# Forty projections of the first attention block on 64-row tiles that swap banks, with one pool of seven PSUM banks and a new order

## The chip, the cores and the metric

The kernel runs on one core of one Trainium2 chip. The metric is the device time of one execution in microseconds, taken as the median of several runs. A profile of one more execution (its "profiled execution") shows what each engine did: TensorE (PE, with its weight loads as PEld), VectorE (DVE), ScalarE (ACT), GpSimd (POOL) and the DMA queue that SyncE issues (SP).

## What is computed

Two independent attention blocks over 2048 tokens of 512 features with 32 heads of 16. Block A sees only the current token and the 255 before it; block B sees all tokens. The outputs stand side by side.

```python
def _A_ref(x, wqkv, wo):          # B, S, D = 1, 2048, 512; H = 32, Dh = 16, W = 256
    qkv = ...((x @ wqkv).reshape(B, S, 3, H, Dh))
    q, k, v = qkv[0], qkv[1], qkv[2]
    scores = jnp.einsum("bhqd,bhkd->bhqk", q, k) * (Dh ** -0.5)
    mask = (idx[:, None] - idx[None, :] >= 0) & (idx[:, None] - idx[None, :] < W)
    scores = jnp.where(mask[None, None], scores, -1e9)
    p = _softmax(scores, axis=-1)
    o = jnp.einsum("bhqk,bhkd->bhqd", p, v)
    return o.transpose(0, 2, 1, 3).reshape(B, S, D) @ wo
# _B_ref: the same without the mask
return jnp.concatenate([a, b], axis=-1)
```

## The kernel before

**Splitting.** Every float32 operand of a projection is held as a rounded part and a remainder (`split`, L136 to L138, or L263 and L264), and a product of two operands is three matmuls: rounded by rounded, rounded by remainder, remainder by rounded. A projection (`project_qk`, `project_v`) contracts 512 features in four pieces of 128 rows, so it is 12 matmuls of 128 x 512, all accumulating in one PSUM bank (`products`, L188). `ps_all` is the whole PSUM as eight banks of 512 columns.

**Layouts on TensorE.** Three layouts of the array occur. Projections use all 128 rows. Scores (L537) and row maxima (L426 for block A, L378 for block B) contract 48 or 51 rows, so two heads stand at partitions 0 and 64 (`ROW = 0, 64`) and run as pairs on two 64-row tiles, each into a bank of its own. Weighing with the values (L583 for A, L568 for B) has 17 output columns, and four heads stand on four 32-column tiles. The transpose of the row maxima (L504, 48 columns) is a fourth. These layouts are called modes below, and a stretch of instructions in one mode a stay.

**Block A's stage.** A loop reads `ORDER_A`, one letter a step: `p` a whole projection, `m` a maximum (two heads of one query tile), `s` scores of two heads, `w` a weighing, `t` the transpose of the finished maxima, `e` a maximum of block B done early. `ORDER_P` names the projections in order (`Aq01`: block A, queries of head group pair 0, token chunk 1; `Av13`: values of token tile 7). All 96 projections of queries, keys and values of both blocks are done in this stage. What else happens (loads, stores, splits) is put in by a planner, `Model`, that keeps a time for each engine and a release time for each bank; the order on each engine is then fixed in the program, and engines wait for one another by semaphores. The planner charges a `turn` when TensorE changes its mode.

**Banks.** Scores take single banks of a pool `e` of three; maxima take double banks of a pool `p` of two; the accumulator of weighings has one bank, `o`. Projections and transposes take `e`, or one half of a `p` before the scores begin. A bank comes free when ACT or DVE has read it: scores by the exponentials (L544), maxima by DVE (L435 then L436, or L382), projections by an ACT copy (L249, L253, L330).

**After a projection.** Queries and keys: ACT copies the bank to `raw` (L253), POOL splits it (L263, L264), SP stores it (L271), and later loads bring it to `oq` and `opk` in the layout of the scores. Values: ACT copies to `vst` (L330), SP stores (L338). Probabilities of block A are masked by POOL (L554) before they are weighed; scores run at most `AHEAD` = 3 steps ahead of weighings.

**Block B's stage** follows, with the fixed pattern `ORDER` of scores, maxima and weighings; `max_rows` (L504) occurs there too.

Of the kernel before, what the change touches and what calls it, by code (L numbers as in the profile page):

```python
# [20 lines left out]
HG = 4  # L21
# [7 lines left out]

NAMES = str.maketrans({"(": "", ")": "", ",": "", " ": "_", "'": ""})  # L30
# [15 lines left out]

ORDER_P = (
# [4 lines left out]
    "Bk12 Bk33 Bk31 Bk30 Bk11 Bq30 Bq13 Bq31 Bq20 Bk32 Bq32 Bq33 ").split()  # L52
# [6 lines left out]
    "ppppppppppmmpmmpmmpmmpmmpmmtppmmpmmspsmmptpmsmswsmmpmsmwsmptmmspmswmsmpsmwsmmpmswsmmpmsmwtsmmswsmpmm"  # L59
    "spmtmswmswsmmpsmwsmmswtmsmpsmwsmmpmswstmmspmswmsmswmsmpmsmwtswsmmswspsmmpmsmwmspsmmwsmtwsmmswmsmpsmw"  # L60
    "mstmpsmmswsmmswsmpsmmwtmspsmwsmmwmswmsmsmpmmswspmtpmsmwswmspmmspsmmstmwsmsmwmsmpmswmmpmsmtsmwmmspsmm"
    "wmstwmssmwmsmsmpmsmwtsmwsmmsmswmsmpmsmwsmsmmwtsmmswmspsmmwsmsmwsmmsptmwmsmpsmwsmmswtmspsmwmsptmmpsmm"
    "wswsmpsmwsmmpmsmwtsmmswmsmpsmmswmsmpmsmwtmswsmwmsmpsmmswsmmswtmsmswmsmpmmswsmpmswtmsmpmsmwsmpsmmwsmp"
    "msmwtsmmswsmpmmswsmpmswtmmspmswmmspmswsmmtpsmmwswesmpmsmwsmpsempesmwtmswmsmpmswmmspemspemtpsewsmmpsm"
    "mwsmpsemwspemspmsmwtsewmsmpsmmwtsesmpesmwsmpmswmsmpsmmwsmpmsmwwmmtpemspesmpesmpemswsmwmswsmmpsempmsm"
    "pmsmptmmwwwmm")
# [7 lines left out]
class Model:  # L74
# [14 lines left out]
    def pe(self, mode, ns, *after):  # L89

        turn = self.turn * (mode != self.mode)
        self.mode = mode
        return self.run("PE", turn + ns, *after)
# [25 lines left out]
def attention_kernel(ctx: ExitStack, tc: tile.TileContext, xT, wqk, wv, wo, out):  # L119
# [62 lines left out]
    def products(ps, pairs, start=True, stop=True):  # L182
# [3 lines left out]
        for l, r in pairs:  # L186
            for u, v in ((0, 0), (0, 1), (1, 0)):
                nc.tensor.matmul(ps, l(u), r(v), start=start and k == 0, stop=stop and k == n - 1)  # L188
                M.pe("f", 232)
# [9 lines left out]
    def view(bank):  # L199
        pool, n = bank  # L200
        first, width = {"e": (0, 1), "o": (3, 1), "p": (4, 2), "s": (6, 1)}[pool]
        n = first + width * n + (pool == "e" and n > 2)
        return ps_all[:, n] if width == 1 else ps_all[:, n:n + 2]

# [13 lines left out]
    def constants():  # L218
# [11 lines left out]
        for v in vt:  # L230
            nc.gpsimd.memset(v[:, :, VP:], 1.0)
# [7 lines left out]

    def project_qk(b, p, s, c):  # L240

        n = f"{b}_{p}_{s}_{c}"
        bank, ps = room()
        yield from products(ps, [(lambda u, i=i: ws[b, p, s][:, u, 128 * i:128 * i + 128], lambda v, i=i: xs[b, c, i][:, v])
                      for i in range(4)])
        at_most(project_qk, 1)
        two = sb.tile([128, 2, QC], F32R, name=f"st_{n}", tag="st")
        if (b, p) == (0, 0):
            nc.scalar.activation(two[:, 0], ps, AF.Copy)  # L249
            t1 = M.run("ACT", 480, M.t["PE"] + WAKE)  # L250
        else:
            raw = row(f"raw_{n}")
            nc.scalar.activation(raw, ps, AF.Copy)  # L253
            t1 = M.run("ACT", 480, M.t["PE"] + WAKE)
# [20 lines left out]
        after(t1, sub, (project_qk, b, p, s, c))  # L275

# [44 lines left out]

    def project_v(b, c, a):

        kt = 4 * c + a
        bank, ps = room()
        yield from products(ps, [(lambda u, i=i: xs[b, c, i][:, u, 128 * a:128 * a + 128], lambda v, i=i: ws[b, "v", i][:, v])
                      for i in range(4)])
        v = vst[0]
        vst.reverse()
        nc.scalar.activation(v[:, :, 0:DH], ps.rearrange("p (h d) -> p h d", d=DH), AF.Copy)  # L330
        t = M.run("ACT", 480, M.t["PE"] + WAKE)
# [35 lines left out]
    def max2(g, c, qt, kc, heads, ps):  # L367
# [14 lines left out]
        nc.vector.tensor_reduce(out=m[:, a:a + len(heads), r, qt, kc], in_=ps, axis=AX.X, op=ALU.max)  # L382
        return M.run("DVE", 65 + 533 * len(heads), t)
# [23 lines left out]
    def max_item(b, g, c, qt, j, kc):  # L407
        n = f"{b}_{g}_{c}_{qt}_{j}_{kc}"
        if b:
            pr = M.take("p")  # L410
            M.release(pr, max2(g, c, qt, kc, (j, j + 1), view(pr)))
            return
# [9 lines left out]
        bank = M.take("p")  # L422
        two = view(bank)
# [5 lines left out]
        if i < 2:  # L429
            for a in range(2):  # L430
                nc.vector.tensor_tensor_reduce(junk[:, :w], two[:, a, 0:w], wmask[:, 256 - w:], 1.0, -3.0e38,
                                               ALU.add, ALU.max, accum_out=m[:, a, r, qt, 0:1])
                t = M.run("DVE", w / 0.96 + 310, t)
        else:
            nc.vector.copy_predicated(two[:, :, 256:384], later, two[:, :, 0:128])  # L435
            nc.vector.tensor_reduce(out=m[:, :, r, qt, 0], in_=two[:, :, 128:384], axis=AX.X, op=ALU.max)  # L436
            M.run("DVE", 455, t)
            t = M.run("DVE", 610)
        M.release(bank, t)
# [25 lines left out]
    def max_finish(b, g, c):  # L465
# [13 lines left out]
        nm = sb.tile([128, 2, 3, HG // 2, 4], BF16, name=f"nm_{n}", tag="nm")  # L479
        parts["nm"] = nm  # L480
        nm = [nm[:, :, i].rearrange("p a r q -> p a (r q)") for i in range(3)]
# [259 lines left out]
    def bank():  # L741
        return M.bank(pool())
# [402 lines left out]
```

## Time and profile before

| | |
|---|---|
| runs | 1834.06 us median of 3 (1833.39 to 1835.33) |
| profiled execution | 1839.76 us, its span on the core 1838.0 us, mean granted TensorE clock 0.994 |
| TensorE busy in the span | 99% |
| block A's stage | from 0 to about 550 us |
| L188 projections of the whole run (`ps_all<-x,w` and `ps_all<-w_v,x`) | 768 and 384 matmuls, mean 408 and 399 ns |

A matmul's length in the profile covers its whole way through the array, and those that follow overlap it; the distance from start to start says what one costs in a row. So the timeline is read by its first column. The groups of instructions by line have, behind the bar, the idle time of the engine before them and what ended it.

### The profile page before, as it was taken

The page shows a single profiled execution, that of the slowest core. Times are in us where ns is not written, and L with a number is a line of the kernel's source. Part 1 is how long each engine was busy: PE and PEld are TensorE (multiplying, and loading weights), DVE is VectorE, ACT ScalarE, POOL GpSimd, SP SyncE. Part 2 cuts the span into 40 slices and gives each one's busy share as a digit, 9 for nine tenths or more (in the row PEclk, how much of TensorE's full clock was granted, in tenths as well). Part 3 has the DMA queues.
Part 4 walks back from the last instruction along what each step waited for, and adds up shares of the span by engine and source line. Part 5 has one row for each costly group of instructions (what it writes and reads, how often), then busy time and mean ns, then how long its engine had stood idle before and what let it go on. Part 6 is the DMA issues. An engine that isn't in the chain of part 4 may idle for free. (4 is left out here: it accounts for less than half of the span.)

```text
span 1838.0 us, 37676 instructions
## 1 busy us (share of the span) xinstructions
PE 1815.5 (99%) x14376; PEld 901.5 (49%) x14376; DVE 1530.6 (83%) x2275; ACT 1404.2 (76%) x2750; POOL 648.8 (35%) x1333
## 2 busy tenths in 40 slices
PE   8999999999999999999999999999999999999999
PEld 6666656666663544444444443444444434444436
DVE  4677677766778777799999999999999999999901
ACT  4366566665547777799999999999999999999983
POOL 0367878564662433032221022430013232122330
PEclk9999999999998999999999999999999999999999
DMA  8755656545554222411310032121031121010012
GB/s 261 206 178 184 208 183 197 165 151 158 167 174 108 85 84 84 98 29 34 63 37 17 23 74 49 28 63 30 17 75 29 34 63 36 17 49 12 32 36 92
DMA packets 129157, 166.72 MB, mean 91 GB/s; under 512 B 23012, under 2 KB 58852, under 8 KB 128964
## 3 DMA queue, kind: packets, MB, share of 16 engines
q1 hardware_dynamic: 128976, 164.31, 30.7%
q8 instruction: 113, 1.85, 0.4%
q14 instruction: 68, 0.56, 0.1%
HBM read 94.49 MB, written 68.19 MB: 89 GB/s over the span
## 5 line engine op out<-in xcount | busy, mean ns | idle before, releaser
L544 ACT ACTIVATE p<-ps_all 128x512 f32<-128x512 f32 x2432 | 1260.7, 597 | 161.1 <-PE ps_all L537 104.8
L382 DVE TENSOR_REDUCE mt<-ps_all 128x2 f32<-128x1024 f32 x1516 | 1195.1, 868 | 77.4 <-PE ps_all L378 73.4
L537 PE MATMUL ps_all<-oq,opk 51*128 51x512 f32 (+2 forms) x2752 | 783.6, 409 | 6.3 <-ACT p L544 5.4
L378 PE MATMUL ps_all<-opk,oq 48*128 48x512 f32 x2016 | 677.5, 440 | 2.1 <-DVE mt L382 1.9
L568 PE MATMUL ps_all<-p,vt 128*17 128x256 f32 (+1 forms) x6056 | 590.6, 462 | 0.5 <-ACT ou L594 0.5
L537 PEld LDWEIGHTS ps_all<-oq,opk 51*128 51x128 f32 x2752 | 400.2, 185 | 193.9 <-ACT p L544 170.8
L378 PEld LDWEIGHTS ps_all<-opk,oq 48*128 48x128 f32 x2016 | 310.3, 186 | 317.8 <-DVE mt L382 177.7
L554 POOL TENSOR_SCALAR_AFFINE_SELECT p<-p 128x256 f32<-128x256 f32 x480 | 179.8, 406 | 148.4 <-ACT p L544 141.8
L568 PEld LDWEIGHTS ps_all<-p,vt 128*17 128x17 f32 x6056 | 101.0, 95 | 225.0 <-issue 214.4
L188 PE MATMUL ps_all<-x,w 128*128 128x512 f32 x768 | 198.3, 408 | 7.1 <-ACT x L137 6.6
L453 POOL TENSOR_TENSOR mu<-mt 128x16 f32<-128x16 f32 x31 | 6.8, 220 | 509.6 <-DVE mt L382 509.6
L435 DVE COPY_PREDICATED ps_all<-mone,ps_all 128x256 f32<-128x256 uint16 x224 | 94.9, 424 | 90.7 <-PE ps_all L426 89.6
L188 PEld LDWEIGHTS ps_all<-x,w 128*128 128x128 f32 x768 | 143.5, 193 | 47.2 <-ACT x L137 6.8
L436 DVE TENSOR_REDUCE mt<-ps_all 128x2 f32<-128x512 f32 x224 | 155.3, 693 | 7.7
L622 POOL TENSOR_TENSOR rd<-ld,minus 128x32 f32<-128x32 f32 x15 | 81.9, 5457 | 220.6 <-DMA ld<-od 220.6
L253 ACT ACTIVATE raw<-ps_all 128x512 f32<-128x512 f32 x56 | 33.5, 598 | 106.5 <-PE ps_all L188 106.5
L583 PE MATMUL ps_all<-p,vt 128*17 128x384 f32 (+2 forms) x1408 | 95.8, 387 | 0.0
L188 PE MATMUL ps_all<-w_v,x 128*128 128x512 f32 x384 | 95.6, 399 | 0.0
L426 PE MATMUL ps_all<-opk,oq 48*128 48x384 f32 (+2 forms) x512 | 91.0, 376 | 2.4 <-DVE mt L436 2.2
L188 PE MATMUL ps_all<-w_o,x_o 128*128 128x512 f32 x384 | 92.8, 396 | 0.1
L188 PEld LDWEIGHTS ps_all<-w_o,x_o 128*128 128x128 f32 x384 | 70.6, 188 | 30.0 <-issue 13.6
L188 PEld LDWEIGHTS ps_all<-w_v,x 128*128 128x128 f32 x384 | 70.0, 188 | 18.7 <-issue 2.7
(72 smaller groups left out, 738.9 us busy)
## 6 DMA issues: line engine op xcount, KB each, us to landing
parts<-st SPq DMA_DIRECT2D x64, 512.0 KB
oq<-parts SPq DMA_DIRECT2D x128, 128.0 KB
opk<-parts SPq DMA_DIRECT2D x128, 128.0 KB
od<-ou SPq DMA_DIRECT2D x64, 256.0 KB
vd<-vst SPq DMA_DIRECT2D x32, 272.0 KB
oq<-parts SPq DMA_DIRECT2D x128, 64.0 KB
opk<-parts SPq DMA_DIRECT2D x128, 64.0 KB
t<-od SPq DMA_DIRECT2D x32, 256.0 KB
```

The costliest lines, as they stand in the source:

```text
L188: nc.tensor.matmul(ps, l(u), r(v), start=start and k == 0, stop=stop and k == n - 1)
L378: nc.tensor.matmul(ps[:, n], q[rows, 128 * qt:128 * qt + 128], k[rows, kc * QC:kc * QC + QC], start=True, stop=True)
L382: nc.vector.tensor_reduce(out=m[:, a:a + len(heads), r, qt, kc], in_=ps, axis=AX.X, op=ALU.max)
L426: nc.tensor.matmul(two[:, a, 0:w], opq[b, g, c][rows, r, 128 * qt:128 * qt + 128], opk2(g)[rows, r, t0:t1], start=True, stop=True)
L435: nc.vector.copy_predicated(two[:, :, 256:384], later, two[:, :, 0:128])
L436: nc.vector.tensor_reduce(out=m[:, :, r, qt, 0], in_=two[:, :, 128:384], axis=AX.X, op=ALU.max)
L537: nc.tensor.matmul(ps[x][:, col:col + n1], opk2(g)[rows, pr, 128 * k:128 * k + 128], opq[b, g, c][rows, pr, q0:q0 + n1], start=True, stop= ...
L544: nc.scalar.activation(p[:, a0 + x, :w], ps[x][:, :w], AF.Exp, scale=SCALE)
L554: nc.gpsimd.affine_select(out=v, in_=v, pattern=[[0, 2], [sign, 128]], compare_op=ALU.is_ge, fill=zero_fill, base=base, channel_multiplier ...
L568: nc.tensor.matmul(o[32 * j:32 * j + VW, q0:q1], vt[(g // 2) % 2][:, kt, vc:vc + VW], pts[1, g, c, kt, j // 2][:, j % 2, q0:q1], start=kt ...
L583: nc.tensor.matmul(o[32 * j:32 * j + VW, q0:q0 + w], vt[(g // 2) % 2][:, kt, vc:vc + VW], pts[b, g, c, m, j // 2][:, j % 2, col:col + w], ...
L622: nc.gpsimd.tensor_tensor(rd, ld, minus, op=ALU.pow)
```

## The change

**Pairs on 64-row tiles.** 40 of the 96 projections are no longer done one by one. Two are taken together (`g` in `ORDER_A`, 80 letters: four chunks for each of 20 pairs). A pair's products are cut in half along the contraction: in the first two chunks, rows 0 to 63 of the first projection run on the upper tile into the first bank, and rows 64 to 127 of the second on the lower tile into the second bank. In the last two chunks the halves are exchanged, so that each tile writes the other bank. One chunk is 6 steps of two matmuls, so a pair is 48 matmuls of 64 rows instead of 24 of 128. Other letters stand between the chunks.

**The wait at the swap.** The first matmul after the exchange is made to depend on the earliest eviction, by the planner's time, of anything that TensorE was given after the first half (`since`, `mark`).

**One pool.** `e` and `p` become one pool `u` of seven single banks; maxima and scores take any two (`take2`, read with a stride), projections and transposes one, a pair two from its first chunk to its evictions. In block B's stage the banks are as before.

**Transposes.** The maxima are kept 32 columns apart with zeros in the unused 8 (`nmt`), and two transposes of 32 columns replace one of 48, in both blocks; the copy behind them has 64 rows for 48.

**Small changes.** One of two constant margins (`vt[0]`) is dropped, the planner's `turn` has one value for each mode, and `ORDER_P` and `ORDER_A` are new throughout.

```diff
+CHUNK = 6
 ORDER_P = (
-    "Aq00 Aq01 Ak00 Av13 Av00 Av03 Aq02 Av20 Ak01 Av10 Av21 Ak02 Av02 Av33 Aq03 Av01 Ak03 Av12 Av11 Aq13 Aq10 "
+    "Aq00 Ak00 Av11 Av01 Aq01 Av03 Ak01 Ak02 Av13 Av12 Aq02 Av00 Aq03 Av02 Av10 Ak03 Av23 Ak11 Av32 Ak10 Av20 "
...
 ORDER_A = (
-    "ppppppppppmmpmmpmmpmmpmmpmmtppmmpmmspsmmptpmsmswsmmpmsmwsmptmmspmswmsmpsmwsmmpmswsmmpmsmwtsmmswsmpmm"
+    "pppppppppmmpmmppmmgmgmpmmgtmgmmpmmgsgmspsmgsmgmswtmmmppmsgsmgmmpsmgmmgmwtwmmspmsgmsgmswsgmsgmtwssmws"
...
-        self.mode, self.turn = "f", 170
-        self.banks = {"e": [0] * 3, "p": [0] * 2, "o": [0]}
+        self.mode, self.turn = "f", dict(f=210, h=200, c=139)
+        self.banks = {"u": [0] * 7, "o": [0]}
...
+    def take2():
+        banks = sorted(M.take("u") for _ in range(2))
+        i, j = (n + n // 3 - n // 6 for _, n in banks)
+        return banks, ps_all[:, i:j + 1:j - i]
...
+    nmt = [cst.tile([128, 2, 32], BF16, name=f"nm{i}") for i in range(2)]
-    vt = [cst.tile([128, NT, VP + 16], F32, name=f"vt{i}") for i in range(2)]
+    vt = [cst.tile([128, NT, VP + 16 * i], F32, name=f"vt{i}") for i in range(2)]
...
+    def mark(op, t):
+
+        since.append((t, len(since), op))
+        return t
+
+    def half_rows(stage, pairs, banks):
+
+        turn, q0 = divmod(CHUNK * stage, 12)
+        for q in range(q0, q0 + CHUNK):
+            k, i = divmod(q, 3)
+            u, v = ((0, 0), (0, 1), (1, 0))[i]
+            for a in range(2):
+                l, r = pairs[a ^ turn][k]
+                rows = slice(64 * a, 64 * a + 64)
+                op = nc.tensor.matmul(view(banks[a ^ turn]), l(u)[rows], r(v)[rows], start=turn == q == 0,
+                                      stop=turn == 1 and q == 11)
+                if turn and q == a == 0:
+                    tc.add_manual_dep(op.ins, min(since)[2].ins.name, LANDED, reason="the row tiles change banks")
+        M.pe("h", CHUNK * 233)
...
-        bank = M.take("p")
-        two = view(bank)
+        banks, two = take2()
...
-        nc.tensor.transpose(ps[:48, :128], nm.rearrange("p a s j q -> p (a s j q)"), ident)
-        nt = sb.tile([48, 128], F32, name=f"ntr_{n}", tag="ntr")
-        nc.scalar.activation(nt, ps[:48, :128], AF.Copy)
+        for a in range(2):
+            nc.tensor.transpose(ps[32 * a:32 * a + 32, :128], nm[:, a], ident)
+        nt = sb.tile([64, 128], F32, name=f"ntr_{n}", tag="ntr")
+        op = nc.scalar.activation(nt, ps[:64, :128], AF.Copy)
...
+        elif x == "g":
+            if stage == 0:
+                two = its_a[nb:nb + 2]
+                nb += 2
+                banks = [M.take("u") for _ in range(2)]
+            half_rows(stage, [(pairs_qk if f == project_qk else pairs_v)(*a) for f, *a in two], banks)
+            stage += 1
+            if CHUNK * stage == 12:
+                since.clear()
+            elif CHUNK * stage == 24:
+                stage = 0
+                for (f, *a), bank_ in zip(two, banks):
+                    (end_qk if f == project_qk else end_v)(*a, bank_, view(bank_))
+                    made.add((f, *a))
```

The order on TensorE shows the change best. The rows are line, operation, output and inputs, columns, and the repeat count. First the program before, early in block A's stage: whole projections (L188) of 12 matmuls between maxima (L426) and a transpose (L504).

```order
L426 MATMUL ps_all<-opk_73,oq_0_1_254 128x384 x4
L188 MATMUL ps_all<-x_3_0_308,w_0_0_113 128x512 x3
L188 MATMUL ps_all<-x_3_1_311,w_0_0_113 128x512 x3
L188 MATMUL ps_all<-x_3_2_325,w_0_0_113 128x512 x3
L188 MATMUL ps_all<-x_3_3_328,w_0_0_113 128x512 x3
L426 MATMUL ps_all<-opk_73,oq_0_1_254 128x384 x4
L504 LDWEIGHTS nm_0_0_451
L504 MATMUL ps_all<-ident,nm_0_0_451 48x128
L188 MATMUL ps_all<-w_v_160,x_0_0_116 128x512 x3
```

After the change, about the same place: the end of a pair's first chunk, one maximum (now L474), and the second chunk (L314); both projections' operands alternate.

```order
L314 MATMUL ps_all<-x_3_1_297,w_0_0_116 128x512
L314 MATMUL ps_all<-w_v_181,x_0_1_122 128x512
L474 MATMUL ps_all<-opk_75,oq_0_0_231 128x384
L474 MATMUL ps_all<-opk_75,oq_0_0_231 128x384 [waits Activation_49]
L314 MATMUL ps_all<-x_3_2_312,w_0_0_116 128x512 [waits DVE_49]
L314 MATMUL ps_all<-w_v_190,x_0_2_127 128x512
```

The same projection of chunk 3 with `w_0_0`, one stay in the full array before, now shares its tiles' mode with the maxima beside it, in pieces.

Later in block A's stage, after the change: the swap of a pair, with the two narrow transposes (L553), scores (L586) and an early maximum of block B (L427) between the halves. The bracket names the engine whose result the first matmul of the second half waits for.

```order
L314 MATMUL ps_all<-w_v_3820,x_2_3_3196 128x512
L553 LDWEIGHTS nm_74
L553 MATMUL ps_all<-ident,nm_74 32x128
L586 MATMUL ps_all<-oq_6_2_4905,opk_75 128x256 [waits Activation_49] x2
L586 MATMUL ps_all<-oq_6_2_4905,opk_75 128x256 x2
L427 MATMUL ps_all<-vt_77,qe 128x512 x2
L314 MATMUL ps_all<-w_v_3579,x_2_0_3055 128x512 [waits Activation_49]
L314 MATMUL ps_all<-x_3_0_3320,w_2_0_4304 128x512
```

Before, no instruction waited for an eviction of another bank in this way, and a transpose never stood between the parts of a projection.

The end of the stage, before: two maxima of block B (L378, two pairs of matmuls), the first scores of block B (L537), and the next maximum.

```order
L583 MATMUL ps_all<-p_7_3_2_1_6468,vt_76 17x128 x2
L378 MATMUL ps_all<-opk_73,oq_0_1_6033 128x512 x4
L537 MATMUL ps_all<-oq_0_0_5866,opk_73 128x512 x2
L378 MATMUL ps_all<-opk_73,oq_0_1_6033 128x512 x2
```

And after, with three maxima and a whole projection there:

```order
L632 MATMUL ps_all<-p_7_3_2_1_6912,vt_78 17x128 x2
L427 MATMUL ps_all<-opk_75,oq_0_1_6513 128x512 x6
L190 MATMUL ps_all<-x_1_0_2633,w_3_1_6262 128x512 x3
L190 MATMUL ps_all<-x_1_1_2672,w_3_1_6262 128x512 x3
L190 MATMUL ps_all<-x_1_2_2754,w_3_1_6262 128x512 x3
L190 MATMUL ps_all<-x_1_3_2775,w_3_1_6262 128x512 x3
L586 MATMUL ps_all<-oq_0_0_6244,opk_75 128x512 x2
```

The last projection moved from before the last weighings to behind the last maxima of the stage.

Counted over TensorE's printed order up to block A's last weighing and what follows it before block B's first weighing, the stays in each mode are:

| mode | before | after |
|---|---|---|
| full array (projections; after: those not paired) | 86 | 46 |
| 64-row tiles | 183 | 135 |
| 32-column tiles (weighings; after: transposes too) | 93 | 93 |
| the transpose's own | 33 | 0 |

Of the 20 swaps, 6 have a wait in their row; at the other 14 TensorE has waited for that result, or a later one of the same engine, at an instruction ahead of the swap.

More of the change, by code (lines that the diff above doesn't have):

```diff
@@ L89, in pe @@
     def pe(self, mode, ns, *after):
-        turn = self.turn * (mode != self.mode)
+        turn = self.turn[mode] * (mode != self.mode)
         self.mode = mode
@@ L200, in view @@
         pool, n = bank
+        if pool == "u":
+            return ps_all[:, n + n // 3 - n // 6]
         first, width = {"e": (0, 1), "o": (3, 1), "p": (4, 2), "s": (6, 1)}[pool]
@@ L409, in max_item @@
         if b:
-            pr = M.take("p")
-            M.release(pr, max2(g, c, qt, kc, (j, j + 1), view(pr)))
+            banks, two = take2()
+            release2(banks, max2(g, c, qt, kc, (j, j + 1), two))
             return
@@ L421, in max_item @@
         w = t1 - t0
-        bank = M.take("p")
-        two = view(bank)
+        banks, two = take2()
         for a in range(2):
@@ L530, in scores @@
         pr, a0 = divmod(j, 2)
-        banks = [M.take("e") for _ in range(heads)]
+        banks = [M.take("e" if b else "u") for _ in range(heads)]
         ps = [view(bank) for bank in banks]
@@ L752, in room @@
             return None, view(("s", slot[1]))
-        while bank() >= M.NEVER:
-            advance()
-        b = M.take(pool())
-        return b, view(b)[:, 0] if b[0] == "p" else view(b)
+        b = M.take("u")
+        return b, view(b)
     def release(b, t):
@@ L928, in load_next @@
         f(*a)
+    stage, two, banks = 0, None, None
     todo_a = list(ORDER_A)
```

109 lines of the change are left out of this document (63 added, 46 removed), and 6 rows, old and new, of the table ORDER_P.

## The prediction

> **What bounds the kernel now.** I read the page first, then the busy time by stretch (columns: busy microseconds and instruction count of each engine, granted TensorE clock, DMA share, GB/s), then the waits of TensorE alone up to 552 us, where the first block ends.
>
> ```profile
> PE 1815.5 (99%) x14376; PEld 901.5 (49%) x14376; DVE 1530.6 (83%) x2275; ACT 1404.2 (76%) x2750; POOL 648.8 (35%) x1333
> ...
> 184.00:230.00 46.00, 44.51 (x327) 28.61 (x327) 28.95 (x69) 26.84 (x55) 37.37 (x65) 0.96 0.67 209
> 230.00:276.00 46.00, 43.28 (x330) 27.00 (x330) 35.26 (x80) 27.94 (x57) 34.14 (x65) 0.96 0.59 182
> 276.00:322.00 46.00, 44.15 (x352) 28.07 (x350) 35.03 (x79) 30.53 (x63) 37.81 (x70) 1.00 0.66 197
> 552.00:598.00 46.00, 45.58 (x328) 18.04 (x332) 40.62 (x53) 35.29 (x69) 14.31 (x27) 0.85 0.42 102
> ...
> 0.00:552.00 552.00, 534.81 (x3891) 352.81 (x3891) 377.94 (x795) 308.32 (x608) 332.24 (x645) 0.99 0.60 186
> 552.00:1838.00 1286.00, 1280.65 (x10485) 548.72 (x10485) 1152.62 (x1481) 1095.92 (x2142) 316.59 (x688) 0.99 0.19 50
> ```
> ```profile
> PE ps_all L188 <- ACT x L137: 6.6, 1, 6.6
> PE ps_all L537 <- ACT p L544: 5.2, 13, 0.7
> PE ps_all L426 <- DVE mt L436: 2.2, 8, 0.6
> PE ps_all L537 <- DMA oq<-ntr: 0.5, 1, 0.5
> PE ps_all L188 <- DVE x L138: 0.2, 1, 0.2
> PE ps_all L188 <- ACT p L544: 0.2, 1, 0.2
> ```
>
> In the first 552 us TensorE is busy for 534.8 and its six kinds of wait add up to 14.9, of which 6.6 is the first load. No other engine is near: DVE 378, POOL 332, ACT 308 of 552. So this block lasts as long as TensorE's instruction stream, and the change must be priced in that stream. After 552 us TensorE is again the fullest (1280.7 of 1286), with DVE behind it (1152.6).
>
> "Busy" hides what matters here. The start times in the timeline (start, length, instruction; the number behind x is how many stand in the row) show it:
>
> ```profile
> 18.30 8.32 PE L188 MATMUL ps_all<-w_v,x 128*128 128x512 f32 x36
> 26.46 2.88 PE L188 MATMUL ps_all<-x,w 128*128 128x512 f32 x12
> ...
> 37.80 2.99 PE L188 MATMUL ps_all<-w_v,x 128*128 128x512 f32 x12
> 40.72 0.51 PE L426 MATMUL ps_all<-opk,oq 48*128 48x256 f32 x4
> 41.16 3.02 PE L188 MATMUL ps_all<-x,w 128*128 128x512 f32 x12
> 44.10 0.62 PE L426 MATMUL ps_all<-opk,oq 48*128 48x384 f32 x4
> ```
>
> Projections in a row take (26.46 - 18.30) / 36 = 0.227 us per matmul, 2.72 per projection. A projection between two 64-row pieces takes 40.72 - 37.80 = 2.92 or 44.10 - 41.16 = 2.94: **0.21 us more for one stay in the full-array mode**. The same for the 64-row mode and for the transpose, later in the trace:
>
> ```profile
> 549.31 0.74 PE L378 MATMUL ps_all<-opk,oq 48*128 48x512 f32 x4
> 549.89 0.46 PE L537 MATMUL ps_all<-oq,opk 51*128 51x512 f32 x2
> 552.27 0.50 PE L378 MATMUL ps_all<-opk,oq 48*128 48x512 f32 x2 [1.93 <-DVE mt L382]
> 552.61 0.40 PE L537 MATMUL ps_all<-oq,opk 51*128 51x512 f32 x2
> 552.85 0.40 PE L378 MATMUL ps_all<-opk,oq 48*128 48x512 f32 x2
> 553.08 0.39 PE L537 MATMUL ps_all<-oq,opk 51*128 51x512 f32 x1
> ...
> 588.08 0.40 PE L378 MATMUL ps_all<-opk,oq 48*128 48x512 f32 x1
> 588.08 0.39 PE L537 MATMUL ps_all<-oq,opk 51*128 51x512 f32 x1
> 588.40 0.62 PE L568 MATMUL ps_all<-p,vt 128*17 128x256 f32 x8
> 588.96 0.24 PE L504 MATMUL ps_all<-ident,nm 128*48 128x128 bf16 x1
> 589.12 0.50 PE L537 MATMUL ps_all<-oq,opk 51*128 51x512 f32 x1
> ```
>
> A 64-row pair of 512 columns starts 0.24 and 0.23 after the one before it (552.61, 552.85, 553.08), but 0.34 after the first pair of a stay (552.27 to 552.61), and the next mode starts 0.32 after the last pair (588.08 to 588.40). So a stay costs 0.10 + 0.09 = 0.19 beside its work. A transpose is a stay of its own: 0.16 from its start to the next mode.
>
> **The change part by part.** Stays are counted in TensorE's printed order up to the block's last weighing. Full-array stays fall from 86 to 46, 64-row stays from 183 to 135, transpose stays from 33 to none; column stays remain 93.
>
> Projections: 40 of them leave the full array, so 40 stays go: 40 x 0.21 = 8.4 saved (bounds 8.0 and 8.8). Their 480 matmuls become 480 pairs of half height. A pair carries 512 columns on 64 rows a tile; the nearest row is the 512-column pair above, 0.23 to 0.24 against 0.227: 480 x 0.008 = 3.8 lost (bounds 1.5 and 6.2).
>
> 64-row stays: the chunks join the scores and maxima beside them, 48 stays fewer: 48 x 0.19 = 9.1 saved (bounds 8.2 and 9.8, from 0.17 to 0.205: the upper one is the stay at 40.72, 0.44 us for two pairs of 256 columns at half of 0.235 each).
>
> Transposes: 33 x 0.16 = 5.3 removed. Two 32-column ones stand inside a column stay instead. The trace has none such; below it is a quarter of a 512-column pair, 0.06, above it is a stay as now, 0.16. I take 0.08, near the lower end, since the order puts them between matmuls of the same 32-column tiles: 33 x 0.08 = 2.6 saved (0 to 3.3). The second block has 31 more, 31 x 0.08 = 2.5 (0 to 3.1); TensorE is full there, so it counts.
>
> Sum of the stream: -8.4 + 3.8 - 9.1 - 2.6 - 2.5 = **-18.8 us**.
>
> The wait at the swap: 20 swaps, but only 6 have a wait in the printed order; in the other 14 TensorE has already waited for a later result. Behind the waiting matmul stand the rest of the pair and all further scores and maxima, so ACT and DVE would run dry in turn. What is waited for is the earliest eviction of anything computed since the first half ended:
>
> ```profile
> L436 DVE TENSOR_REDUCE mt<-ps_all 128x2 f32<-128x512 f32 x224 | 155.3, 693 | 7.7
> L435 DVE COPY_PREDICATED ps_all<-mone,ps_all 128x256 f32<-128x256 uint16 x224 | 94.9, 424 | 90.7 <-PE ps_all L426 89.6
> L382 DVE TENSOR_REDUCE mt<-ps_all 128x2 f32<-128x1024 f32 x40 | 47.6, 1223 | 27.8 <-PE ps_all L378 27.5
> ...
> L544 ACT ACTIVATE p<-ps_all 128x512 f32<-128x512 f32 x322 | 175.0, 597 | 38.3 <-PE ps_all L537 28.7 <-PE ps_all L426 2.0 <-POOL p L554 1.7
> L253 ACT ACTIVATE raw<-ps_all 128x512 f32<-128x512 f32 x56 | 33.5, 598 | 106.5 <-PE ps_all L188 106.5
> ...
> L264 POOL TENSOR_TENSOR st<-raw,st 128x512 fp32r<-128x512 f32 x56 | 71.9, 1285 | 4.7
> L263 POOL CAST st<-raw 128x512 fp32r<-128x512 f32 x56 | 34.2, 611 | 8.6 <-DMA parts<-st 6.0 <-ACT raw L253 2.6
> ```
>
> That is 0.60 on ACT or 0.42 + 0.69 = 1.11 on DVE, while in every case shown TensorE has a transpose, scores, a maximum or a weighing to do meanwhile. Bounds 0 and 6 x 1.1 = 6.6; I take 1.2.
>
> The pool: no instruction is added, but a pair holds two of seven banks through all four chunks and leaves five, where scores had three and maxima two pairs. Now those waits are 5.2 + 2.2; I add 2 (bounds -4 and the rival below).
>
> What moves with a pair: its two evictions come together (2 x 0.60 on ACT), then two splits on POOL (2 x 1.90), which stand ahead of the masks in POOL's queue, then two stores of 512 KB on SP's queue ahead of the loads queued there. ACT (56% busy) covers the first. POOL has 82% in its fullest stretch (276 to 322 us), so a weighing there may come 1.9 later than with single projections; scores run three steps ahead of weighings, which covers it. I price it at nothing; uncovered it is rival one. At the opening, values come third instead of fourth:
>
> ```profile
> 15.38 2.49 DVE L138 TENSOR_TENSOR w_v<-in_v,w_v 128x512 fp32r<-128x512 f32 x4
> ```
>
> Their weights are ready at 17.87; with the last three matmuls behind that (3 x 0.227), the third projection ends at 18.6, where it now ends at 18.30: 0.3 lost.
>
>  The wider zeroed rows and the smaller constant tile are off TensorE.
>
> The boundary: now TensorE waits 1.93 at 552.27 because two 1.22 us reductions follow the last scores with nothing between, and the clock falls to 0.85 in that stretch. In the new order a projection (2.7 us) follows three such maxima (3.7 us): the wait should shrink to 1 us, so -1; of the clock I take nothing for sure.
>
> Total: -18.8 + 1.2 + 2 + 0.3 - 1 = -16.3. With the lost clock, 46 x (0.04 + 0.04 + 0.15) = 10.6 us now, more likely to shrink than to grow, I take -2.5 more: **-19 us**. The profiled execution took 1839.76 (span 1838.0), 5.7 above the median of the runs, 1834.06; terms of the stream are the same in both, so 1834 - 19 = **1815**, and about 1821 if profiled.
>
> **The rivals.** *One: given back to another engine.* POOL at 82%, DVE's bursts or the loads turn into waits and eat 12 of the 19: 1827. For it: DVE has two or three maxima in a row of 1.11 each against 1.41 of chunk. Against: 552-us totals of 378 and 332 leave a third of each engine free.
>
> *Two: five banks are too few* (slower). A maximum holds two banks for its pair and 1.11 of DVE, two scores hold two for 2 x 0.60 of ACT; one chunk of 6 x 0.235 = 1.41 just covers one of them, and with five banks a third unit must wait. At 60 gaps inside pairs, 0.5 us each is 30 us: 1815 + 30 = 1845. It decides from 19 / 60 = 0.3 us a gap. For it: already now 13 waits reach up to 0.7 us. Against: those sum to 5.2 with even fewer single banks for scores, and ACT and DVE drain at the same time.
>
> *Three: half-height matmuls don't overlap.* If each extra matmul takes time of its own, the bound is half of a 128-column pair, about 0.03 us: 480 x 0.03 = 14 us, less the 3.8 already counted: 1825. Against: both of a pair start at 588.08. The Trainium skill speaks for this rival and against the change: "TensorEngine Tiling (Array Packing)", When to Use Tiling, recommends row tiles for contractions of 64 or fewer, and its Instruction Overhead gives every matmul about 60 cycles. At the 2.4 GHz of "TensorE: Matmul & The Clock Gate" that is, as an estimate from these pages, 480 x 25 ns = 12 us, and the sum would be -11 instead of -19. The trace disagrees: 0.23 to 0.24 for a pair, against 0.227 for one matmul of 128 rows.
>
> *Four: more.* Most of the 10.6 us of lost clock goes too: 1804.
>
> **How the numbers follow.** Forecast 64% (1806 to 1823), rival one 14%, two 9%, three 5%, four 8%. A measurement of this kernel can tell 0.2%, 3.7 us. Faster: 64 + 8 + 9 of rival one + 4 of three = 85; same: 5 + 1 = 6; slower: rival two, 9. The range 1803 to 1831 holds the forecast, nearly all of one and three and half of four, less the tails: about 8 in 10.
>
> **What would show it.** In the profile after: chunk matmuls 0.23 to 0.24 apart in pairs; no 0.10 and 0.09 around a chunk; the last weighing of the first block near 534 us instead of 549; TensorE's waits there still near 15 us; the two narrow transposes 0.06 to 0.1 long with no stay of their own. Wrong if waits on L436 or L544 exceed 25 us up to the boundary (rival two), if pairs stand 0.26 apart (three), or if POOL is named as releaser of the weighings (one).

## The result, and the profile after

| | before | after |
|---|---|---|
| runs, measured together | 1833.26 us median of 6 (1831.69 to 1835.33) | 2182.84 us median of 6 (2173.6 to 2192.42) |
| profiled execution | 1839.76 us, span 1838.0 | 2192.42 us, span 2190.7 |
| mean granted TensorE clock | 0.994 | 0.913 |
| first weighing of block B | 556.9 us | 912.1 us |
| block B's stage from there to the end | 1281.2 us | 1278.6 us |

The ratio is 1.1908, with a 95% interval of 1.1885 to 1.1931. The change makes the kernel 19% slower, and all of it happens in block A's stage, which becomes 355 us longer.

From the page of the kernel after, the busy time of each engine and the granted clock in 40 slices:

```profile
PE 1947.2 (89%) x14920; PEld 982.5 (45%) x14920; DVE 1529.3 (70%) x2275; ACT 1404.4 (64%) x2750; POOL 650.0 (30%) x1334
...
PEclk9977788669778768799999999999999999999999
```

The work of DVE, ACT and POOL is what it was (1530.6, 1404.2 and 648.8 before). Only TensorE takes longer. The busy time by stretch (columns as in the prediction):

```profile
46.00:92.00 46.00, 31.51 (x197) 21.77 (x197) 19.64 (x40) 10.41 (x23) 8.14 (x15) 0.93 0.45 130
...
460.00:506.00 46.00, 32.05 (x199) 20.47 (x201) 15.90 (x31) 12.91 (x28) 16.24 (x29) 0.67 0.46 131
...
0.00:905.00 905.00, 668.19 (x4399) 434.47 (x4400) 377.04 (x795) 306.44 (x604) 330.38 (x643) 0.80 0.37 114
905.00:2190.00 1285.00, 1279.02 (x10522) 548.03 (x10521) 1152.31 (x1480) 1097.94 (x2146) 319.62 (x691) 1.00 0.18 49
```

TensorE stands idle for 905 - 668.2 = 236.8 us, where before it was 552 - 534.8 = 17.2: 219.6 more. It is busy for 668.2 instead of 534.8, 133.4 more, at a mean clock of 0.80 instead of 0.99. The two make 353 of the 355. Nothing else is near its limit: DVE is busy for 377 of 905 us.

The waits of TensorE up to 905 us (in all, times, longest):

```profile
PE ps_all L586 <- DVE mt L484: 58.0, 36, 2.5
PE ps_all L474 <- DVE mt L484: 38.4, 27, 2.4
PE ps_all L632 <- DVE mt L484: 36.3, 22, 3.1
PE ps_all L314 <- DVE mt L484: 30.9, 19, 2.4
PE ps_all L190 <- DVE mt L484: 15.0, 9, 2.5
PE ps_all L314 <- DVE mt L431: 12.7, 7, 2.2
PE ps_all L632 <- POOL p L603: 7.3, 3, 2.6
```

Before, L436 (now L484) held TensorE for 2.2 us in 8 waits. Now every kind of instruction waits for it: scores (L586), maxima (L474), weighings (L632), chunks (L314), whole projections (L190). A weighing reads probabilities and writes the accumulator's bank, and a chunk writes two banks that its pair already holds; neither needs anything from a maximum. The timeline of TensorE shows the rhythm:

```profile
44.99 0.44 PE L474 MATMUL ps_all<-opk,oq 48*128 48x384 f32 x2
47.04 0.45 PE L474 MATMUL ps_all<-opk,oq 48*128 48x384 f32 x2 [1.61 <-DVE mt L484]
47.33 0.39 PE L314 MATMUL ps_all<-x,w 64*128 64x512 f32 x1
...
47.56 0.39 PE L314 MATMUL ps_all<-x,w 64*128 64x512 f32 x1
...
48.72 0.34 PE L474 MATMUL ps_all<-opk,oq 48*128 48x384 f32 x2
50.34 0.50 PE L314 MATMUL ps_all<-x,w 64*128 64x512 f32 x1 [1.28 <-DVE mt L484]
...
53.40 3.01 PE L190 MATMUL ps_all<-w_v,x 128*128 128x512 f32 x12 [1.25 <-DVE mt L484]
```

and that of DVE in the same microseconds:

```profile
45.83 0.43 DVE L483 COPY_PREDICATED ps_all<-mone,ps_all 128x256 f32<-128x256 uint16 x1 [2.08 <-ACT vst L379]
46.29 0.69 DVE L484 TENSOR_REDUCE mt<-ps_all 128x2 f32<-128x512 f32 x1
...
49.13 0.43 DVE L483 COPY_PREDICATED ps_all<-mone,ps_all 128x256 f32<-128x256 uint16 x1 [0.44 <-PE ps_all L474]
49.59 0.69 DVE L484 TENSOR_REDUCE mt<-ps_all 128x2 f32<-128x512 f32 x1
```

A reduction ends at 46.29 + 0.69 = 46.98 and TensorE goes on at 47.04; the one at 49.59 ends at 50.28 and TensorE goes on at 50.34. After a maximum TensorE waits until DVE has read it, 1.25 to 1.6 us in these rows, and DVE in turn waits for the next maximum. The two engines take turns.

**The first theory.** A maximum's two banks are now any two of seven, read by DVE through one view with a stride (`ps_all[:, i:j + 1:j - i]` in `take2`). The program's dependencies take such a view as the whole stretch from its first bank to its last. So TensorE waits at every bank that lies in between, though DVE does not touch it. Counted over the built programs, TensorE's waits for a DVE result in block A's stage:

| kernel | writes a bank that the DVE instruction reads | writes a bank that only lies between |
|---|---|---|
| before | 269 | 0 |
| after | 57 | 164 |

The row quoted ahead of the prediction, `x_3_2_312,w_0_0_116 128x512 [waits DVE_49]`, is one of the 164: it writes bank 4, and the reduction that it waits for reads banks 0 and 6. The view of waits puts 219 us on L484 and L431, in 139 waits of 1.6 us on average. The count shows which banks are concerned, not that this is what costs the time; that is for the experiments.

### The profile page after: what moved, and what is told of

It is laid out like the page before. It is cut to its first block, busy times and chain, and to the rows that moved or that the text cites. A ratio compares the mean times of both kernels' runs of the same rounds, so it can differ in the third digit from the quotient of the medians.

```text
span 2190.7 us, 39133 instructions
## 1 busy us (share of the span) xinstructions
PE 1947.2 (89%) x14920; PEld 982.5 (45%) x14920; DVE 1529.3 (70%) x2275; ACT 1404.4 (64%) x2750; POOL 650.0 (30%) x1334
## 3 DMA queue, kind: packets, MB, share of 16 engines
q8 instruction: 118, 1.93, 0.4%
## 5 line engine op out<-in xcount | busy, mean ns | idle before, releaser
L431 DVE TENSOR_REDUCE mt<-ps_all 128x2 f32<-128x1024 f32 x1516 | 1196.2, 866 | 133.7 <-PE ps_all L427 78.6
L586 PE MATMUL ps_all<-oq,opk 51*128 51x512 f32 (+2 forms) x2752 | 794.8, 422 | 67.3 <-DVE mt L484 58.0
L427 PE MATMUL ps_all<-opk,oq 48*128 48x512 f32 x2016 | 678.7, 440 | 6.4 <-DVE mt L431 6.4
L586 PEld LDWEIGHTS ps_all<-oq,opk 51*128 51x128 f32 x2752 | 411.4, 196 | 265.1 <-ACT p L593 154.7
L427 PEld LDWEIGHTS ps_all<-opk,oq 48*128 48x128 f32 x2016 | 310.6, 185 | 322.6 <-DVE mt L431 184.7
L314 PE MATMUL ps_all<-x,w 64*128 64x512 f32 x624 | 155.3, 464 | 26.6 <-DVE mt L484 16.1
L190 PE MATMUL ps_all<-x,w 128*128 128x512 f32 x456 | 156.5, 508 | 19.4 <-DVE mt L484 11.4
L632 PE MATMUL ps_all<-p,vt 128*17 128x384 f32 (+2 forms) x1408 | 123.7, 478 | 49.1 <-DVE mt L484 36.3
L484 DVE TENSOR_REDUCE mt<-ps_all 128x2 f32<-128x512 f32 x224 | 155.1, 693 | 7.7
L474 PE MATMUL ps_all<-opk,oq 48*128 48x384 f32 (+2 forms) x512 | 115.1, 431 | 41.4 <-DVE mt L484 38.4
L190 PEld LDWEIGHTS ps_all<-x,w 128*128 128x128 f32 x456 | 111.2, 252 | 56.2 <-issue 9.5
L314 PEld LDWEIGHTS ps_all<-x,w 64*128 64x128 f32 x624 | 103.7, 222 | 43.8 <-DVE mt L484 18.5
L314 PE MATMUL ps_all<-w_v,x 64*128 64x512 f32 x336 | 105.0, 452 | 17.1 <-DVE mt L484 14.9
L474 PEld LDWEIGHTS ps_all<-opk,oq 48*128 48x128 f32 x512 | 62.8, 223 | 89.5 <-issue 39.6
```

What stands on the lines that cost most here:

```text
L314: op = nc.tensor.matmul(view(banks[a ^ turn]), l(u)[rows], r(v)[rows], start=turn == q == 0, stop=turn == 1 and q == 11)
L427: nc.tensor.matmul(ps[:, n], q[rows, 128 * qt:128 * qt + 128], k[rows, kc * QC:kc * QC + QC], start=True, stop=True)
L431: op = nc.vector.tensor_reduce(out=m[:, a:a + len(heads), r, qt, kc], in_=ps, axis=AX.X, op=ALU.max)
L474: nc.tensor.matmul(two[:, a, 0:w], opq[b, g, c][rows, r, 128 * qt:128 * qt + 128], opk2(g)[rows, r, t0:t1], start=True, stop=True)
L484: op = nc.vector.tensor_reduce(out=m[:, :, r, qt, 0], in_=two[:, :, 128:384], axis=AX.X, op=ALU.max)
L586: nc.tensor.matmul(ps[x][:, col:col + n1], opk2(g)[rows, pr, 128 * k:128 * k + 128], opq[b, g, c][rows, pr, q0:q0 + n1], start=True, stop= ...
```

## The experiments

Each kernel was run beside the kernel before on the same chip; the chips differ between experiments, and the last column shows how well they agree. **Time at full clock** below is the mean over a kernel's runs of its time multiplied by its mean granted clock, an estimate of what it would take if the throttle granted everything; for kernels in which TensorE mostly waits (after, e3) it is only rough. Over the runs of one kernel it scatters by 1 to 2 us (standard deviation; after: 4), less than the times do: beside e8, runs of the kernel before at clock 0.998 took about 1831, at 0.996 about 1835, and both give 1827.

| kernel | median us | ratio (95%) | mean clock | full clock, us | before beside it |
|---|---|---|---|---|---|
| after | 2182.84 | 1.1908 (1.1885 to 1.1931) | 0.917 | 2001.2 | |
| e1_neighbours | 1846.18 | 1.0074 (1.0057 to 1.0091) | 0.990 | 1827.0 | 1828.5 |
| e2_one_bank_reads | 1839.99 | 1.0045 (1.0031 to 1.0059) | 0.993 | 1825.2 | 1828.5 |
| e3_old_kernel_spread_banks | 2029.02 | 1.1074 (1.1055 to 1.1093) | 0.970 | 1968.1 | 1828.5 |
| e4_narrow_transposes_alone | 1833.20 | 0.9999 (0.9990 to 1.0008) | 0.997 | 1827.0 | 1828.5 |
| e5_full_height_chunks | 1860.53 | 1.0133 (1.0102 to 1.0163) | 0.993 | 1848.8 | 1827.7 |
| e7_pool_with_old_order | 1838.07 | 1.0025 (1.0012 to 1.0039) | 0.997 | 1833.3 | 1827.7 |
| e8_replanned | 1831.16 | 0.9990 (0.9981 to 1.0000) | 0.994 | 1820.9 | 1827.4 |
| e9_split_later | 1832.75 | 0.9998 (0.9988 to 1.0008) | 0.993 | 1819.8 | 1827.7 |

### Two neighbouring banks

```diff
-        banks = sorted(M.take("u") for _ in range(2))
-        i, j = (n + n // 3 - n // 6 for _, n in banks)
-        return banks, ps_all[:, i:j + 1:j - i]
+        t, i, j = near()
...
+        n = i + i // 3 - i // 6
+        return [("u", i), ("u", j)], ps_all[:, n:n + 2]
+
+    def near():
+        u = M.banks["u"]
+        return min((max(u[i], u[j]), i, j) for i, j in ((0, 1), (1, 2), (3, 4), (4, 5), (5, 6)))
```

Pairs of projections take two neighbours too. Expected:

> The changed kernel, but a maximum (and a pair of projections) takes two neighbouring banks instead of any two, so that what VectorE reads in one instruction has no other bank in between; order, pairs and swap waits stay. Theory A (TensorE is made to wait for VectorE at every bank that lies between the two that a maximum uses, since the two-bank view is taken as one stretch of banks): the waits on the maxima's reductions fall from some 200 us to under 25 us, the clock of block A's stage returns to 0.95 or more, and the time to 1805 to 1835 us, where the prediction had it. Theory B (five banks beside a pair are too few): fewer choices of banks make it no better, 2150 us or more. Theory C (the waits at the bank swap hold TensorE): they are all still there, 2100 us or more.

Measured: 1846.18 us. Of the 350 us, 337 are gone, with the same seven banks, orders, chunks and swaps. TensorE's largest waits up to 552 us:

```profile
PE ps_all L480 <- DVE mt L490: 7.9, 12, 2.3
PE ps_all L190 <- ACT x L139: 7.3, 2, 7.0
PE ps_all L480 <- ACT p L599: 3.2, 9, 0.5
```

The program has 272 waits on an own bank and none on one between. But the kernel is still slower than the one before, and above the 1805 to 1835 us that theory A gave.

### The spread banks, read one at a time

```diff
-            nc.vector.copy_predicated(two[:, :, 256:384], later, two[:, :, 0:128])
-            op = nc.vector.tensor_reduce(out=m[:, :, r, qt, 0], in_=two[:, :, 128:384], axis=AX.X, op=ALU.max)
+            for a in range(2):
+                nc.vector.copy_predicated(two[:, a, 256:384], later[:, a], two[:, a, 0:128])
+                op = nc.vector.tensor_reduce(out=m[:, a, r, qt, 0:1], in_=two[:, a, 128:384], axis=AX.X, op=ALU.max)
```

The early maxima of block B are split in the same way; banks and orders are those of after. Expected:

> The changed kernel with its own choice of banks, but in block A's stage VectorE reads each of a maximum's two banks by instructions of its own (two predicated copies and two reductions instead of one and one). Same order, same planner, same banks. Theory A: no view spans a bank that is not its own, so the waits go although nothing about the banks has changed: 1820 to 1870 us, above the kernel with neighbours because VectorE has some 60 us more of instructions in this stage. Theory B and C: VectorE is slower and banks come free later, 2200 us or more.

Measured: 1839.99 us. So the spread banks themselves cost nothing; one instruction over two of them does. DVE pays for the split, as its groups of instructions by line and form show:

```profile
L489 DVE TENSOR_REDUCE mt<-ps_all 128x1 f32<-128x256 f32 x448 | 190.4, 425 | 15.4
L488 DVE COPY_PREDICATED ps_all<-mone,ps_all 128x128 f32<-128x128 uint16 x448 | 129.2, 288 | 42.4 <-PE ps_all L478 39.2 <-PE ps_all L591 1.9 <-PE ps_all L314 0.3
```

319.6 us for what took 155.3 + 94.9 = 250.2 before. These 69 us of DVE cost TensorE little: its waits on L489 are 5.9 us in all up to 552 us, and e2 is 6 us faster than e1, where it was expected to be slower.

### The old kernel with spread banks

The kernel before, with one rule changed: its two double banks in block A's stage are 4 and 6, and 5 and 7, instead of 4 and 5, and 6 and 7.

```diff
+        if pool == "p" and not slot[0]:
+            n = 4 + bank[1]
+            return ps_all[:, n:n + 3:2]
         return ps_all[:, n] if width == 1 else ps_all[:, n:n + 2]
```

Expected:

> The kernel before, with one difference: in block A's stage the two double banks of the maxima are 4 with 6 and 5 with 7 instead of 4 with 5 and 6 with 7. No pairs, no pool, no new order, as many banks. Theory A: each maximum now waits for the one before it, whose view spans one of its banks; with 224 and 40 maxima at about 1 us each, less what stands between them, the time rises by 80 to 250 us, to 1910 to 2080 us. Theory B and C: no bank is fewer and there is no swap, so 1830 to 1837 us.

Measured: 2029.02 us, 196 us more with nothing else changed. First its row in the waits up to 552 us, then its timeline:

```profile
PE ps_all L429 <- DVE mt L439: 88.7, 84, 2.3
```
```profile
60.44 0.44 PE L429 MATMUL ps_all<-opk,oq 48*128 48x384 f32 x2
62.16 0.44 PE L429 MATMUL ps_all<-opk,oq 48*128 48x384 f32 x2 [1.27 <-DVE mt L439]
```

The same 1.27 us after a maximum, in a kernel without chunks, pool or new order. Counted as above, its program has 9 waits on an own bank and 262 on one that only lies between. The theory of the view stands.

### The narrow transposes alone

The kernel before with `nmt`, the two 32-column transposes and the smaller margin, and nothing else of the change.

```diff
-        nc.tensor.transpose(ps[:48, :128], nm.rearrange("p a s j q -> p (a s j q)"), ident)
+        for a in range(2):
+            nc.tensor.transpose(ps[32 * a:32 * a + 32, :128], nm[:, a], ident)
```

Expected:

> The kernel before with nothing but the two 32-column transposes for one of 48 (and the wider zeroed rows). By the prediction's term 64 x 0.08 = 5.1 us less, 1828 us; by its lower bound nothing, 1833 us; by its upper bound 6.4 us less. It does not bear on theories A, B and C.

Measured: no difference in time (0.9990 to 1.0008), and 1.5 us less at full clock, where 5.1 were expected. The timelines say why. Before, the 48-column transpose and what follows; then the two narrow ones, at the same place:

```profile
55.17 0.24 PE L504 MATMUL ps_all<-ident,nm 128*48 128x128 bf16 x1
55.34 3.02 PE L188 MATMUL ps_all<-w_v,x 128*128 128x512 f32 x12
```
```profile
54.55 0.23 PE L507 MATMUL ps_all<-ident,nm 128*32 128x128 bf16 x2
54.71 3.02 PE L188 MATMUL ps_all<-w_v,x 128*128 128x512 f32 x12
```

0.17 and 0.16. Two narrow transposes cost what one wide one does, and they are still a stay of their own unless a weighing stands beside them. The 15 in block A that follow a weighing start 0.11 us sooner after it than before; block B's 31 follow one too, but gain only 0.02 each (median 0.455 instead of 0.476 from the last weighing to the next scores).

### Full-height chunks

e1 with every chunk as six matmuls of 128 rows, in the same places (half a projection a chunk, no swap).

```diff
-            for a in range(2):
-                l, r = pairs[a ^ turn][k]
-                rows = slice(64 * a, 64 * a + 64)
-                op = nc.tensor.matmul(view(banks[a ^ turn]), l(u)[rows], r(v)[rows], start=turn == q == 0,
-                                      stop=turn == 1 and q == 11)
...
+            l, r = pairs[turn][k]
+            nc.tensor.matmul(view(banks[turn]), l(u), r(v), start=q == 0, stop=q == 11)
```

Expected:

> The neighbours kernel (e1), with the chunks at the same places, but each is 6 full-height matmuls of one projection instead of 6 pairs of half height of two: the first projection fills the first two chunks, the second the last two, and no swap and no wait at it is left. The planner is charged as before, so the order is that of e1. Theory D (a change of mode is worth what the prediction took from the trace, and half-height pairs run at 0.23): each of the 80 chunks becomes a full-array stay of its own, with its entry and exit and those of the 64-row stay that it cuts, 80 x (0.20 + 0.19) = 31 us, less 480 x 0.004 = 2: e1 plus 29, 1875 us. Theory E (the pairs give nothing, modes cost nothing where TensorE waits anyway): within 8 us of e1, 1838 to 1854 us.

Measured: 1860.53, 14 more than e1, half of what was expected. At full clock it is 1848.8 - 1827.0 = 21.8 more. Its timeline:

```profile
46.80 0.45 PE L475 MATMUL ps_all<-opk,oq 48*128 48x384 f32 x2
47.18 1.64 PE L318 MATMUL ps_all<-x,w 128*128 128x512 f32 x6
48.75 0.44 PE L475 MATMUL ps_all<-opk,oq 48*128 48x384 f32 x2
```

Six matmuls take 48.75 - 47.18 = 1.57 where 6 x 0.227 = 1.36 would do: 0.21 for the stay. In the timeline of after a chunk takes 48.72 - 47.33 = 1.39. So half-height pairs do save the stays, in about the predicted amount; summed over the trace the stays of e5 cost 25 to 32 us more than those of e1, depending on what is counted as a stay's own work (an estimate from the start times). That TensorE waits less where such stays cover ACT and DVE explains little of what is missing to 21.8: behind the opening it waits 15 us in e5 and 18 in e1. Between 21.8 and the 14 that were measured lies the clock (0.993 against 0.990).

### The pool with the old order

e1 with the tables `ORDER_P` and `ORDER_A` of the kernel before, so one pool and narrow transposes, but no pairs. Expected:

> The neighbours kernel (e1) with the old order: no pairs, 96 whole projections, the old letters, but the pool of seven with neighbours and the narrow transposes. Theory F (what e1 lost against the kernel before is the price of the pool under the neighbour rule, whatever the order): slower than before by 5 to 15 us, 1837 to 1847 us. Theory G (the loss of e1 lies in the new order, written for a pool that gives any two banks): no slower than before, 1826 to 1835 us.

Measured: 1838.07, and at full clock 1833.3, 5.6 above the kernel before, as theory F had it. With neighbours demanded of one pool, the order made for three singles and two doubles fits less well; that is a loss of the pool under this rule, apart from the pairs.

### An order made for neighbours

e1 with new tables, searched with the kernel's own planner under the rule that a maximum's banks are neighbours. The first line of one of them:

```diff
-    "pppppppppmmpmmppmmgmgmpmmgtmgmmpmmgsgmspsmgsmgmswtmmmppmsgsmgmmpsmgmmgmwtwmmspmsgmsgmswsgmsgmtwssmws"
+    "pppppppppmmmpmmppmgmmpmgmtmgmmpmmggmsgsmpsmgmgsmpmmwtpmsgmgsmpsmgmmgmsmwtwsmmpmsgmsgmswsmgsmgmmwtwms"
```

Expected:

> The kernel e1_neighbours (two neighbouring banks for each maximum, score pair and projection pair) with new tables ORDER_A and ORDER_P, searched with the kernel's own planner under the rule that two banks must be neighbours; nothing else differs. Theory: e1 gave back its mode saving (about 23 us of turns fewer in block A's stage) because its order had been written for a pool that hands out any two banks; with an order made for neighbours the 64-row items' waits go back to about the 20 us of the kernel before and half clock stays under 20 us, and the time is 1812 to 1828 us, faster than both kernels. Rival: runs of short maxima and scores with chunks between them wait for VectorE and ScalarE in any order, since the full-array stays that used to cover them are gone; then the time is 1833 to 1848 us, no faster than before, with waits of TensorE up to the last weighing of block A still 15 us above the kernel before or half clock over 30 us. Between 1828 and 1833 the order is worth part of it.

Measured: 1831.16, between the theory's range and the rival's. At full clock it is 1820.9, 6.5 below the kernel before and 6.1 below e1; but the clock is 0.994 against 0.997, and 5 us of the 6.5 go there. In the profiled run the last weighing of block A starts at 540.9 instead of 549.1. At the opening of block B a new wait stands in the timeline:

```profile
576.78 0.62 PE L622 MATMUL ps_all<-p,vt 128*17 128x256 f32 x8
581.91 0.29 PE L558 MATMUL ps_all<-ident,nm 128*32 128x128 bf16 x2 [4.51 <-POOL nm L544]
```

TensorE arrives at the first transpose of block B before POOL has its input, because two normalisations of block A's outputs (3.2 us each) stand ahead in POOL's queue.

### That wait taken away

```diff
-        t2 = max(M.dma(256, t1), M.dma(256, t1)) + 2000
+        t2 = max(M.dma(256, t1), M.dma(256, t1)) + (2000 if b else 8000)
```

Expected:

> e8_replanned with one constant changed: the planner lets the normalisation and splitting of block A's outputs (L716 to L719 on GpSimd, 3.2 us each) come 6 us later, so that in GpSimd's queue the second of them no longer stands ahead of the last maxima of block B's first row-maximum unit (L508 to L544). In e8 TensorE waits 4.51 us for L544 at 581.9 us, a wait that the kernel before does not have, and one half-clock spell of 6.8 us follows. Theory: e8 ends block A's stage 8 us earlier than the kernel before in the profiled runs, and gives back at the opening of block B what GpSimd cannot deliver earlier; with the split later that wait falls to about 1 us and the time to 1824 to 1829 us (3.3 us of wait, up to 3.4 of lost clock, against e8's 1831). Rival: VectorE, with 39.6 of the first 46 us of block B's stage busy, is what is late there; the wait moves to its reductions and the time stays 1830 to 1833.

Measured: 1832.75. The waits of TensorE from 530 to 700 us:

```profile
PE ps_all L591 <- DMA oq<-ntr: 2.2, 1, 2.2
PE ps_all L558 <- POOL nm L544: 1.2, 1, 1.2
```

The wait fell from 4.5 to 1.2 us, as the theory had it, and the rival's wait on DVE did not come. Yet the time did not follow: 1.1 us came at full clock, and the mean clock is 0.993 instead of 0.994, which costs 2.3. Both kernels lie within 0.2% of the one before, and both intervals reach 1; neither beats it by what a measurement can tell.

## Why the prediction was wrong, by its steps

**The step that failed** is the one on the pool: "no instruction is added, but a pair holds two of seven banks through all four chunks and leaves five ... I add 2 (bounds -4 and the rival below)". It priced the number of banks and left out how they are read. The line `ps_all[:, i:j + 1:j - i]` stood in the diff, and the printed order above shows its effect: the row `x_3_2_312,w_0_0_116 128x512 [waits DVE_49]` has a matmul of a pair waiting for DVE, with nothing that it could need from there. The price of a wait at every maximum was at hand: 0.42 + 0.69 = 1.11 us of DVE behind each of 224 maxima, uncovered, is 249 us. Measured were 219 us of waits, and 133 us more of busy time at the slower clock behind them.

**Rival two** (slower, 9%) named the right sign and the right test (waits on the maxima above 25 us up to the boundary), by the wrong mechanism; that its test was met is luck. Five banks beside a pair are enough: e2 has the pairs and the spread banks, and its waits on L489 are 5.9 us. The sign of rival one, POOL as releaser of weighings, was there too (7.3 us in 3 waits), but small beside the 219.

**The full-array stays and 64-row stays** (-8.4 and -9.1) were right in the trace. Summed start to start outside half-clock spells (an estimate), entering and leaving modes cost about 73 us in the kernel before, 52 in e2, 50 in e1 and 54 in e8: 19 to 23 less, where -8.4 - 9.1 - 2.6 = -20.1 was predicted. Not the saving failed but the belief that it would all arrive. When block A's last weighing starts, with half clock counted at a half, e2 is 9 us ahead of the kernel before, e1 5 and e8 12 (estimates from the profiled executions). Much of the rest lies between the scores and maxima: from start to start within their stays, with half clock again at a half, they take 111 us before, 124 in e2, 129 in e1 and 121 in e8, of which an estimated 4 only come from there being fewer stays.

**Half height** (+3.8): chunk pairs start 0.231 apart (47.33 to 48.72 for six), not 0.235, so 480 x 0.004 = 1.9 lost. Rival three, and the estimate drawn beside it from "TensorEngine Tiling (Array Packing)", Instruction Overhead, of the Trainium skill (12 us for 480 more instructions), are refuted by that.

**Transposes** (-2.6 and -2.5): mis-sized. The assumed 0.08 is 0.16, the upper bound, where no weighing stands beside; block B's 31, between a weighing and scores, gained 0.02 each instead of 0.08. -5.1 becomes about 0 with an interval of -1.8 to +1.5 (e4's times 1833), and -1.5 at full clock.

**The swap** (+1.2): less. Waits of TensorE at the chunks' matmuls are 0.1 us in all up to the last weighing in e2 and 0.6 in e1.

**The pool, without its view** (+2): the old order loses 5.6 us at full clock with it (e7), an order made for it wins 6.5 (e8). It depends on the order, which the change had made for a pool that hands out any two banks.

**The boundary** (-1) and what moves with a pair (nothing): the boundary's wait did not shrink. Where the kernel before waits 1.93 us for a reduction, e8 and e9 wait 2.2 for the loads of block B's row maxima, and the 4.5 us behind POOL in e8 are rival one's mechanism at a place that it did not name.

**The clock** (-2.5): the wrong sign in every kernel with chunks. The mean share granted is 0.990 to 0.994 in e1, e2, e8 and e9, against 0.996 to 0.998 before. Of e8's gain of 6.5 us at full clock 4.8 are lost so. **Rival one**'s 7 us that arrive were closest for the change without the view, and with the clock less than 2 are left.

What stays open: which pattern of work brings on the half-clock spells. In the main it is not the chunks' matmuls themselves. In e1 four of the seven spells that begin in the stage, 27 of its 48 us at half clock, lie between 229.9 and 301.7 us, and no chunk runs from 105 to 308 us. Here is the busy time of the chunks' matmuls alone (L320; PE and PEld with their counts, then clock, DMA share and GB/s):

```profile
184.00:230.00 46.00, 0.00 (x0) 0.00 (x0) 1.00 0.69 206
230.00:276.00 46.00, 0.00 (x0) 0.00 (x0) 0.85 0.50 157
```

In e5, with full-height chunks, the same four spells begin at the same places of the order, to within four matmuls, and are as long. So the height of the chunks does not bring these on, and that e5's mean clock is higher than e1's (0.993 against 0.990) says little: e5's four runs reach from 0.988 to 0.997. The spells come with the order: e7, with the old one on the same banks, has hardly any (0.997), but what in the new orders causes them no run shows.

## What to carry to other kernels

Look at every wait in a changed program and ask what value it delivers: a wait without one can come from how a view is written down, and in this program one instruction over two separate banks waits, and is waited for, as if it covered all that lies between. A free choice of banks, a view over two of them and an order searched by a planner are one thing: the planner must know the rule by which the program will wait, or its order is wrong by as much as the change can bring (e1 and e8, which differ in their order alone, are 15 us apart). And where TensorE is the bound, set the time times the granted clock beside the time: it tells a saving that was not made from one that was made and lost to the clock.

## What was not expected of the hardware

**Half clock without idle windows.** After, from 460 to 506 us, TensorE is busy for 32.05 of 46 us and the granted clock is 0.67; in block A's stage 379 us pass at half clock (before: 20.5), though behind the opening no wait is longer than 3.1 us. In e2, whose longest wait there is 0.9 us, 20.5 us still do; in e1 it is 47.8 (spells that begin in the stage, from the clock's records of the profiled execution). The spells in the clock's records last 3.41 us or a multiple. The Trainium skill, "TensorE: Matmul & The Clock Gate", Part 1, gives half rate after at least one idle window of about 3.4 us. The length agrees; that a whole window must be idle does not: in e1 and e2 spells begin behind windows of that length with 0.3 to 0.6 us without a running matmul. Nor is that time alone the rule: other windows of e1, on the same grid, have up to 1.3 us of it and are not followed by half clock.

**Two narrow transposes cost what one costs** (0.162 us to the next mode against 0.167), so the price lies in the change of mode and not in the second start. Behind them a weighing, which has the same 32-column tiles, starts after 0.02 us; e8's timeline:

```profile
540.03 0.23 PE L558 MATMUL ps_all<-ident,nm 128*32 128x128 bf16 x2
540.05 1.08 PE L637 MATMUL ps_all<-p,vt 128*17 128x384 f32 x16
```
